# An FFT filter followed by a routed mixture of experts on one core: two input buffers, stores on ScalarE's DMA ring, a padded scratch layout, and six instead of five batches finished after the transform

## The chip, the cores and the metric

The kernel runs on one core of a Trainium2 chip. The metric is device time in microseconds (us) of one execution; the kernel before was timed three times. TensorE (PE) multiplies matrices and writes PSUM; VectorE (DVE), ScalarE (ACT) and GpSimd (POOL) work elementwise, and POOL does not read PSUM here; SyncE (SP) only issues DMAs. SP, ACT and POOL each own a DMA queue, in which their DMAs are issued in program order.

## What is computed

The input x has 8 batches of 2496 rows and 256 columns. Each column of each batch is filtered in the frequency domain, and the 19968 filtered rows then go through a layer of 8 experts with a fixed capacity of 2496 rows each:

```python
X = np.fft.rfft(x, axis=1)
y = np.fft.irfft(X * F, n=x.shape[1], axis=1)     # F = filt_r + 1j*filt_i
logits = y.reshape(B*S, D) @ w_gate
# the largest (row, expert) logits first; an expert that is full takes no more rows
h = np.maximum(x[mask] @ w1[e], 0.0)
out[mask] = h @ w2[e]
```

## The kernel before

**The transform.** 2496 is split as 39 x 64. For each batch `load_x` brings x in three DMAs (L186), one per third of the columns: 39 rows of the first index go to 39 partitions, so a third is 39 x 64 pieces of 86 numbers (344 bytes), and the tile `xt` has 117 partitions. There is one `xt` buffer (22 KB in each partition). `cp_x` (L188 to L195) turns the tile round into `xr0` and `xr1`, two copies each, on DVE (for batch 0 half of them on ACT). `s1` (L207) is the 39-point transform on PE, its results leave PSUM through ACT and DVE (L215). `s2` (L222) is the 64-point transform, followed on DVE by two products with the filter (L228, L229) and on POOL by a difference and a sum (L230, L231). `tr` (L241) transposes the product, `split` makes a high and a low part (ACT L256, DVE L257), L250 and `trv` (L263) prepare the logits. `inv1` (L271) is the first step of the inverse transform: for each q of 0 to 9 it makes a tile `zt` of two values of k1, copied out of PSUM by DVE for even q and ACT for odd q (L283), and stores it to the scratch `zd` in DRAM with two DMAs of 64 partitions (L285), on SP's queue for batches 0 to 6 and ACT's for batch 7. `zt` has 4 buffers.

**The last step.** `load_z` (L357, L359) reads `zd` back in units of five groups of 120 rows (five units per batch, the last with two groups), and `inv2` (L386 to L389) multiplies each with the constant cD (40 or 120 rows by 117), the result leaves PSUM on L390 into `xo`, and L393 stores it to the scratch `xs`, from which the experts gather their rows.

**Order.** `run` gives each call a slot and a priority, a batch being 10 slots, and writes the program in that order; a scheduler with a timing model may move instructions within it, the queues then run in order. With o = 10b, `s1` of batch b stands at slots o-10 to o, `cp_x` of the next batch at o-4.4 and o-0.3, `load_x` of batch b+2 at o-0.2, after the second `cp_x` that empties the single buffer. The last step of batches 0 and 1 stands at slots 18 to 26 and 28 to 36, that of batch 2 (`B - NPOST - 1`) at slots 75 to 83. The other NPOST = 5 batches, 25 units, are worked off in `after()` behind the transform, while the routing looks for the first expert's threshold in 11 rounds of counting (L550 to L610, PE L558 and L571). In that stretch PE's order is written by hand: `Pump` asks for a round each time enough PE work was put between, and units that are left over follow when the first 512 places are known (`for c in units: pass`, L996). The gather of the first expert's rows (L814) and its weights (L793, L999) need all stores to `xs`.

**The experts.** From there on PE multiplies gathered rows with w1 (L850) and w2 (L899), for 8 experts in turn, with the routing of the next expert beside it. The change leaves this part alone, but for two formulas of row numbers.

Memory: the pool `zp` (three `z`, two `xo` buffers) is there from the start; the pool `fx` with `xt` and `xr` is given back at slot 70.5 (`freed`).

Of the kernel before, what the change touches and what calls it, by code (L numbers as in the profile page):

```python
# [15 lines left out]
G = 22  # L16
# [3 lines left out]
NPOST = 5  # L20
# [24 lines left out]
def constants():  # L45
# [4 lines left out]
    cD = np.zeros((120, 117))  # L50
    for b in range(3):
        cS1[39*b:39*b+39, 40*b:40*b+40] = np.concatenate([c, -s], 1)
        cD[40*b:40*b+40, 39*b:39*b+39] = np.concatenate([c, -s], 1).T
# [30 lines left out]
    row[:, 32], row[:, 33], row[:, 34] = p, 64 * (p % 39) + p // 39, p // 39  # L84
# [13 lines left out]
    return dict(cS1=cS1.astype(f), cD=cD.astype(f), cW=cW.astype(f), cEh=Eh, cEl=_round(E - Eh),  # L98
# [4 lines left out]
class Fft:  # L103


    def __init__(s, tc, i, xs, zd, lg, pp, zp):
        s.tc, s.nc, s.i, s.xs, s.zd, s.lg, s.pp, s.zp = tc, tc.nc, i, xs, zd, lg, pp, zp
        s.zw = s.zo = s.y7 = None
# [124 lines left out]
    def tr(s, b, q):  # L233
# [8 lines left out]
        if b == B - 1 and q > 4:  # L242
            nc.scalar.copy(s.y7[:, 2*q:2*q+2], p)
        else:
            s.split(b, q, p, nc.vector)
        if k:
# [5 lines left out]
            nc.scalar.copy(s.vs[b, g], p)  # L252

# [19 lines left out]
    def inv1(s, b, q):  # L273

        nc = s.nc
        if (b, q) not in s.yd:
            s.split(b, q, s.y7[:, 2*q:2*q+2], nc.gpsimd)
        zt = s.wp.tile([128, 2, D], F32, name="zt", bufs=ZB)
# [5 lines left out]
        for r in range(2):  # L284
            (nc.scalar if last else nc.sync).dma_start(s.zd[b][:, 20*r+2*q:20*r+2*q+2], zt[64*r:64*r+64])  # L285
# [5 lines left out]
    def v1(s, g, b0, b1):  # L291

        nc = s.nc
        if s.y7 is None:
            s.y7 = s.wp.tile([128, K1, D], F32, name="Y1", tag="Y1", bufs=2)
# [7 lines left out]
        z = s.y7[r, :10].rearrange("p k d -> p (k d)").rearrange("p (n r k) -> p k r n", r=2, k=K1)[:, 4*g:4*g+4]  # L303
        nc.scalar.copy(z, p[:c].rearrange("p k (r n) -> p k r n", r=2))

    def v2(s, b0, b1):
# [3 lines left out]
        z = s.y7[r, :10].rearrange("p k d -> p (k d)")  # L310
        s.U = s.zp.tile([120, G, c], F32, name="xo", tag="xo", bufs=2)
        n = 8 if c > 8 else G
        for g0 in range(0, G, n):
            g1 = min(g0 + n, G)
            p = s.pt([128, g1 - g0, c], not b0)
            for g in range(g0, g1):
                m = 120 if g < 21 else 40
                nc.tensor.transpose(p[:m, g-g0], z[:, 120*g:120*g+m], s.id[r, r])
            m = min(g1, 21)
            nc.vector.tensor_copy(s.U[:, g0:m], p[:120, :m-g0])  # L320
            if g1 == G:
                nc.vector.tensor_copy(s.U[:40, 21], p[:40, 21-g0])

    def v3(s, b0, b1):
# [3 lines left out]
        for g0 in range(0, G, n):  # L328
            g1 = min(g0 + n, G)
            m = min(g1, 21)  # L330
            p = s.pt([128, g1 - g0, c], not b0)
            nc.tensor.matmul(p[:117, :m-g0], s.cD, s.U[:, g0:m], start=True, stop=True)
            if g1 == G:
                nc.tensor.matmul(p[:117, 21-g0], s.cD[:40], s.U[:40, 21], start=True, stop=True)
            nc.vector.tensor_copy(s.lg[:, b0:b1, g0:g1], p[:117].rearrange("p g (b e) -> p b g e", e=8))

    def more_z(s, units):
# [4 lines left out]
        s.xos = [y[:117, k] for k in range(4)]  # L342
# [8 lines left out]
    def load_z(s, b, t, z=None):  # L351
        g0, gf = 5*t, min(5*t+5, 21)
        if z is None:
            z = s.new_z((b, t) in s.rest)
        s.z[b, t] = z
        v = s.zd[b].rearrange("n k c -> (n k) c")
        s.nc.sync.dma_start(z[:, :gf-g0], v[120*g0:120*gf].rearrange("(g p) c -> p g c", p=120))  # L357
        if t == 4:
# [766 lines left out]
```

## Time and profile before

| what | us |
|---|---|
| median of 3 runs (1575.35 to 1582.28) | 1579.18 |
| the profiled execution, its own time | 1580.15 |
| span of that execution in the trace | 1578.4 |
| from the span's start to the first matmul of the transform | 30.65 |
| from the first matmul of the second batch to the last batch's s1 | 66.08 to 326 |
| the last batch's s1 | 326 to 377 |
| rest of the transform, to the first threshold round | 377 to 449.7 |
| threshold, 25 units of the last step, first gather | 449.7 to 533.7 |
| the experts | 533.7 to 1578 |

The table cuts the span into stages by what PE does. The profile's page gives each engine's busy time over the whole span and in 40 equal slices; the timeline gives instructions in order of time, with the idle time before them in brackets and what ended it; the waits view sums such idle time by pairs. The granted clock of PE is a share of full speed.

### The profile page before, as it was taken

The numbers are of one execution on the slowest core, as the hardware profiler recorded it, in microseconds if no ns is written. First come the engines' busy times: TensorE is split into PE (matmuls) and PEld (weight loads), VectorE is DVE, ScalarE is ACT, GpSimd is POOL, SyncE is SP. The second block draws the span as 40 slices with busy tenths as digits, with TensorE's granted clock in tenths as the row PEclk, the third lists the DMA queues.
The fourth block names the chain that finished last, engine by engine and source line by source line (L and its number), as shares of the span: only waits on it lengthen the run. The fifth ranks groups of instructions, "written<-read, shape, count | busy, mean of one in ns | idle before, by whom it ended". The sixth has DMA issues, their size and how long they took to land.

```text
span 1578.4 us, 27475 instructions
## 1 busy us (share of the span) xinstructions
PE 1419.3 (90%) x10374; PEld 1240.7 (79%) x10374; DVE 979.5 (62%) x2620; ACT 727.5 (46%) x1703; POOL 537.5 (34%) x557
## 2 busy tenths in 40 slices
PE   2788779799898689999999989999999999999998
PEld 1687658689664378888878878888879889899898
DVE  2677556588544856876776686786696772622322
ACT  4465445566444642643553453453462453632322
POOL 0233223335210242354264434343433443333311
PEclk9899989899979789999999999999999999999999
DMA  8878898845878510211121211211211221111100
GB/s 151 146 111 170 189 186 131 170 93 141 190 217 278 185 53 21 88 59 33 71 63 43 77 45 50 79 51 43 89 44 40 92 98 41 48 44 41 47 28 26
DMA packets 121096, 148.75 MB, mean 94 GB/s; under 512 B 70629, under 2 KB 93755, under 8 KB 118659
## 3 DMA queue, kind: packets, MB, share of 16 engines
q1 hardware_dynamic: 97994, 70.63, 22.6%
q0 software_dynamic: 17840, 60.34, 11.8%
q10 hardware_dynamic: 5129, 16.01, 2.9%
q8 instruction: 82, 1.34, 0.4%
q14 instruction: 51, 0.42, 0.1%
HBM read 84.47 MB, written 62.50 MB: 93 GB/s over the span
## 4 chain that ended last, share of the span: by engine, by line
PE 43%; DVE 10%; issue 7%; ACT 2%; POOL 1%; DMA 1%; another core or an unknown queue 0%; POOLq 0%; DVEq 0%; ACTq 0%
PE py L899 20%; PE pz L850 19%; PE rt L558 2%; PE ptr L828 2%; DVE hl L864 1%; POOL out L910 1%; ACT lg L718 1%; DVE hl L867 1%; DVE w0l L808 1%; DVE w1l L808 1%; DMA wr<-moe_w,widx 1%; DVE Gm L550 1%; DVE OH L749 1%; PE rt L755 1%; DVE tmp L639 0%
## 5 line engine op out<-in xcount | busy, mean ns | idle before, releaser
L899 PE MATMUL py<-w1h,hl 128*128 128x256 f32 x2496 | 485.6, 287 | 3.3 <-DVE hl L867 2.8
L899 PEld LDWEIGHTS py<-w1h,hl 128*128 128x128 f32 x2496 | 403.3, 192 | 7.5 <-DVE hl L867 3.7
L899 PE MATMUL py<-w1l,hl 128*128 128x256 f32 (+1 forms) x1280 | 360.1, 283 | 0.0
L910 POOL DMA_INDIRECT out<-y,oid x160 | 173.7, 1086 | 452.3 <-ACT y L909 410.5
L856 ACT ACTIVATE hl<-pz 128x512 fp32r<-128x512 f32 (+1 forms) x320 | 186.4, 587 | 218.1 <-PE pz L850 182.2
L850 PE MATMUL pz<-xo,w0h 128*128 128x512 f32 (+1 forms) x640 | 265.4, 415 | 12.3 <-DVE hl L864 6.7
L850 PE MATMUL pz<-xo,w0l 128*128 128x512 f32 (+1 forms) x640 | 250.1, 391 | 0.0
L850 PE MATMUL pz<-z,w0h 128*128 128x512 f32 (+1 forms) x640 | 249.3, 389 | 0.8 <-DVE z L832 0.8
L899 PEld LDWEIGHTS py<-w1l,hl 128*128 128x128 f32 (+1 forms) x1280 | 242.3, 189 | 2.0
L864 DVE SCALAR_TENSOR_TENSOR hl<-pz,hl 128x512 fp32r<-128x512 f32 x227 | 155.0, 687 | 121.0 <-ACT hl L856 119.5
L814 POOL DMA_INDIRECT xg<-xs,xid x160 | 171.4, 1071 | 134.3 <-issue 43.3
L909 ACT COPY y<-py 128x256 f32<-128x256 f32 x152 | 56.3, 371 | 294.5 <-PE py L899 254.5
L850 PEld LDWEIGHTS pz<-xo,w0h 128*128 128x128 f32 x640 | 122.7, 192 | 33.6 <-DVE hl L864 9.0
L207 PE MATMUL p<-cS,xr 117*128 117x120 f32 x688 | 102.2, 293 | 42.5 <-ACT xr L195 30.7
L850 PEld LDWEIGHTS pz<-xo,w0l 128*128 128x128 f32 x640 | 121.4, 190 | 24.1
L215 ACT COPY Y<-p 64x240 f32<-64x240 f32 (+1 forms) x304 | 116.0, 381 | 44.0 <-PE p L207 38.3
L850 PEld LDWEIGHTS pz<-z,w0h 128*128 128x128 f32 x640 | 122.3, 191 | 17.3 <-DVE z L832 1.8
L207 PEld LDWEIGHTS p<-cS,xr 117*128 117x128 f32 x688 | 94.0, 208 | 49.0 <-ACT xr L195 30.6
L230 POOL TENSOR_TENSOR P<-P 128x256 f32<-128x256 f32 x80 | 59.7, 746 | 209.6 <-DVE P L228 209.2
L550 DVE TENSOR_TENSOR Gm<-M,thr 117x1232 bf16<-117x1232 f32 (+2 forms) x80 | 104.4, 1316 | 0.2
L222 PE MATMUL p<-cW,Y 128*128 128x128 f32 x640 | 92.9, 280 | 1.3 <-DVE Q L229 1.2
L222 PEld LDWEIGHTS p<-cW,Y 128*128 128x128 f32 x640 | 82.9, 194 | 7.8 <-issue 3.7
(234 smaller groups left out, 2255.8 us busy)
## 6 DMA issues: line engine op xcount, KB each, us to landing
xt<-x SPq DMA_DIRECT2D x24, 838.5 KB
zd<-zt SPq DMA_DIRECT2D x140, 128.0 KB
z<-zd SPq DMA_DIRECT2D x26, 600.0 KB
xs<-xo SPq DMA_DIRECT2D x12, 585.0 KB
xs<-xo ACTq DMA_DIRECT2D x11, 585.0 KB
xs<-Y ACTq DMA_DIRECT2D x9, 585.0 KB
zd<-zt ACTq DMA_DIRECT2D x20, 128.0 KB
xg<-xs,xid POOLq DMA_INDIRECT x160
```

What stands on the lines that cost most here:

```text
L207: s.lastmm = nc.tensor.matmul(p[:, q-q0, :120], xv[:, q-24*h], s.cS1, start=True, stop=True).ins
L215: (nc.vector.tensor_copy if t in ((5,) if b else (1, 3, 5, 7, 9)) else nc.scalar.copy)(dst, src)
L222: nc.tensor.matmul(p[:, k], s.Y1[b][:, 4*g+k, dh*128:dh*128+128], s.cW[:, 4*g+k], start=True, stop=True)
L230: nc.gpsimd.tensor_tensor(P[:, :, :64], P[:, :, :64], P[:, :, 64:], op=OP.subtract)
L550: nc.vector.tensor_tensor(Gm[:, s0:s1, :m], s.M[:, s0:s1].unsqueeze(2).to_broadcast([117, s1 - s0, m]), thr[:117].unsqueeze(1).to_broadcas ...
L814: s.lastg = s.nc.gpsimd.indirect_dma_start(out=xg[:n], out_offset=None, in_=s.xs, in_offset=bass.IndirectOffsetOnAxis(ap=ids[0][:n, t:t+1] ...
L850: nc.tensor.matmul(p[:, :n], w[:, sl], x[:, k, :n], start=m == 0, stop=m == 5)
L856: s.lasta = nc.scalar.activation(h[:, :n], p[:, :n], AF.Relu).ins
L864: nc.vector.scalar_tensor_tensor(l[:, :n], p[:, :n], 0.0, h[:, :n].bitcast(F32), op0=OP.max, op1=OP.subtract)
L899: nc.tensor.matmul(p[:a.stop-a.start], hs[g][f][:, a], b[:, 256*f:256*f+256], start=m == 0, stop=m == 8 * len(terms) - 1, skip_group_check ...
L909: s.lasta = nc.scalar.copy(y, p).ins
L910: st = nc.gpsimd.indirect_dma_start(out=out_rows, out_offset=bass.IndirectOffsetOnAxis(ap=ids[1][:w, 4*g+t:4*g+t+1], axis=0), in_=y[:w], i ...
```

## The change

There are six parts.

- **x**: two `xt` buffers; each x is loaded in six parts, and of each third of 39 partitions 32 go in DMAs of 32 partitions, the other seven in one DMA each (one partition, 64 pieces of 344 bytes), 21 per batch. The parts of x for batch b+2 are asked for at slots o-9 to o-3. Batch 0 has three large DMAs on SP's queue and its 21 small ones on ACT's.
- **cp_x**: the first half stands at o-2 (o-4.4 before); one of the four copies of a batch moves from DVE to POOL.
- **stores**: `zt` holds four k1 and has two buffers; each pair of q is stored by two DMAs, all on ACT's queue; the stores of `xs` stand on ACT's queue throughout.
- **scratch layout**: `zd` is 40 x 66 rows, two of 66 being padding that is set to zero by eight small DMAs on SP; a unit of z is then 120 partitions with one run of 5 KB each. cD is 120 x 120, `xs` has 120 rows where it had 117, and the special case of the last group is gone.
- **the last step**: NPOST is 6. The last step of batches 0 and 1 stands at slots 62 to 69, 0.8 slots a unit, its `z` and `xo` cut out of the x buffer that is no longer used; `after()` gets 30 units.
- **memory**: `zp` is opened in `freed`.

```diff
-NPOST = 5
+NPOST = 6
...
-I1, FS, C0 = 5, -1, -4.4
+I1, C0, EZ = 5, -2, 0.8
...
-NP, NZ, MZ, NXO, ZB, NH = 5, 4, 8, 4, 4, 10
+NP, NZ, MZ, NXO, ZB, NH = 5, 4, 8, 4, 2, 10
...
-        s.nz, s.st_x = 3, tc.nc.sync
+        s.nz, s.st_x = 3, tc.nc.scalar
...
+        q = s.wp.tile([128, 4, D], F32, name="zt", bufs=ZB)
+        nc.gpsimd.memset(q[:, :2], 0.0)
+        for zd in s.zd:
+            nc.sync.dma_start(zd[:, N2:], q[:40, :2])
...
-    def load_x(s, b):
-        x = s.i['x'][b]
-        xt = s.xp.tile([128, N2, 86], F32, name="xt", bufs=1)
-        s.xt[b] = [(xt[:117], 0, N2)]
-        xv = x.rearrange("(a c) d -> a c d", c=N2)
-        for k in range(3):
-            s.nc.sync.dma_start(xt[39*k:39*k+39], xv[:, :, 85*k:85*k+86])
+    def load_x(s, b, j):
+
+        if j == 0:
+            xt = s.xp.tile([128, N2, 86], F32, name="xt", bufs=2)
+            s.xt[b] = [(xt[:117], 0, N2)]
+        xt = s.xt[b][0][0]
+        xv = s.i['x'][b].rearrange("(a c) d -> a c d", c=N2)
+        k, h = divmod(j, 2)
+        n, d = slice(32*h, 32*h+32), slice(85*k, 85*k+86)
+        if b == 0:
+            if h == 0:
+                s.nc.sync.dma_start(xt[39*k:39*k+32], xv[:32, :, d])
+            for a in range(32 + 4*h, 36 + 3*h):
+                s.nc.scalar.dma_start(xt[39*k+a:39*k+a+1], xv[a:a+1, :, d])
+            return
+        s.nc.sync.dma_start(xt[39*k:39*k+32, n], xv[:32, n, d])
+        for a in range(32 + 4*h, 36 + 3*h):
+            s.nc.sync.dma_start(xt[39*k+a:39*k+a+1], xv[a:a+1, :, d])
...
-                eng = s.nc.scalar.copy if c and b == 0 else s.nc.vector.tensor_copy
+                eng = (s.nc.scalar.copy if b == 0 else s.nc.gpsimd.tensor_copy if h else s.nc.vector.tensor_copy) if c else s.nc.vector.tensor_copy
...
-        zt = s.wp.tile([128, 2, D], F32, name="zt", bufs=ZB)
+        if q % 2 == 0:
+            s.zt = s.wp.tile([128, 4, D], F32, name="zt", bufs=ZB)
+        zt = s.zt[:, 2*(q % 2):2*(q % 2)+2]
...
-        for r in range(2):
-            (nc.scalar if last else nc.sync).dma_start(s.zd[b][:, 20*r+2*q:20*r+2*q+2], zt[64*r:64*r+64])
+        if q % 2:
+            for r in range(2):
+                nc.scalar.dma_start(s.zd[b].rearrange("a n c -> n a c")[:N2, 20*r+2*q-2:20*r+2*q+2], s.zt[64*r:64*r+64])
...
-        s.nc.sync.dma_start(z[:, :gf-g0], v[120*g0:120*gf].rearrange("(g p) c -> p g c", p=120))
-        if t == 4:
-            s.nc.sync.dma_start(z[:40, 1], v[2520:])
+        s.nc.sync.dma_start(z[:, :g1-g0], s.zd[b].rearrange("a (i g) c -> (a i) g c", i=3)[:, g0:g1])
+
+    def early(s):
+
+        x = s.xp.tile([128, N2, 86], F32, name="xt", bufs=2).rearrange("p n d -> p (n d)")
+        s.ex = [x[:120, 1280*k:1280*k+1280].rearrange("p (g d) -> p g d", d=D) for k in range(4)]
...
             if b + 2 < B:
-                at(o - 0.2, 8, s.load_x, b + 2)
+                for j in range(6):
+                    at(o - 9 + 1.2*j if b else -0.2 + 1.1*j, 8, s.load_x, b + 2, j)
...
-            for t in range(5):
-                if b < B - NPOST:
-                    z = 10*B - I2 if b == B - NPOST - 1 else o + 18
-                    at(z - 2.5 + 2*t, 6, s.load_z, b, t)
-                    at(z + 2*t, 5, s.inv2, b, t)
+        at(10*B - 20, 0, s.early)
+        for k in range(5 * (B - NPOST)):
+            at(10*B - 17.99 + EZ*(k - 2), 9, s.load_z, k // 5, k % 5)
+            at(10*B - 18 + EZ*k, 5, s.inv2, k // 5, k % 5)
...
-        zd = [dr.tile([N2, 40, D], F32, name=f"zd{b}") for b in range(B)]
-        xs = dr.tile([117 * S, D], F32, name="xs")
+        zd = [dr.tile([2 * K1, 3 * G, D], F32, name=f"zd{b}") for b in range(B)]
+        xs = dr.tile([120 * S, D], F32, name="xs")
...
+            f.zp = pool(st, "zp", side="right", reuse_waits="tile")
```

## Rows read from the trace of the kernel before

**Rows 1.** The page: busy time of the engines, then 40 equal slices of the span.
```profile
PE 1419.3 (90%) x10374; PEld 1240.7 (79%) x10374; DVE 979.5 (62%) x2620; ACT 727.5 (46%) x1703; POOL 537.5 (34%) x557
...
PE   2788779799898689999999989999999999999998
...
PEclk9899989899979789999999999999999999999999
DMA  8878898845878510211121211211211221111100
```

**Rows 2.** Windows by stage: length, PE, PEld, DVE, ACT, POOL busy (count), clock, DMA share, GB/s.
```profile
66.08:326.00 259.92, 212.79 (x1842) 190.94 (x1843) 171.94 (x267) 139.90 (x352) 76.84 (x103) 0.89 0.82 155
326.00:377.00 51.00, 50.50 (x524) 47.73 (x523) 41.82 (x71) 35.67 (x91) 22.72 (x30) 1.00 0.35 80
377.00:449.70 72.70, 64.76 (x577) 51.82 (x576) 41.26 (x82) 37.41 (x76) 22.75 (x42) 0.88 0.81 201
449.70:533.70 84.00, 67.92 (x305) 37.79 (x304) 49.37 (x197) 44.01 (x99) 9.08 (x9) 0.87 0.80 257
533.70:1578.00 1044.30, 1000.29 (x6979) 891.43 (x6979) 649.97 (x1950) 443.91 (x1029) 402.24 (x362) 0.99 0.17 55
```

**Rows 3.** Timeline of PE: start, length, instructions, [idle before, what ended it].
```profile
30.65 3.77 PE L207 MATMUL p<-cS,xr 117*128 117x120 f32 x16 [30.65 <-ACT xr L195]
...
66.08 3.77 PE L207 MATMUL p<-cS,xr 117*128 117x120 f32 x16 [9.34 <-DVE xr L195]
...
97.66 0.58 PE L271 MATMUL pa<-yh,cEh 128*128 128x256 f32 x1 [5.88 <-DVE zt L283]
...
176.24 1.09 PE L241 MATMUL pa<-fid,P 128*128 128x128 f32 x4 [7.99 <-ACT Vh L265]
...
230.07 1.12 PE L241 MATMUL pa<-fid,P 128*128 128x128 f32 x4 [9.00 <-DVE xo L390]
...
317.11 1.11 PE L241 MATMUL pa<-fid,P 128*128 128x128 f32 x4 [7.51 <-DVE zt L283]
```

**Rows 4.** Waits up to 620 us: who waited for whom: total us, times, longest.
```profile
DVE xr L195 <- DMA xt<-x: 44.9, 6, 16.5
...
ACT zt L283 <- DMA zd<-zt: 27.5, 4, 9.7
...
DVE zt L283 <- DMA zd<-zt: 14.1, 3, 9.0
```

**Rows 5.** Timeline of SP's DMA issues at the start.
```profile
1.23 12.56 SPq L186 DMA_DIRECT2D xt<-x  x3
...
24.16 0.24 SPq L148 DMA_DIRECT2D P<-filt_r  x1
...
34.01 47.56 SPq L186 DMA_DIRECT2D xt<-x  x6
```

**Rows 6.** Windows in which x alone, and stores of zt alone, are moved (columns of rows 2).
```profile
72.00:87.00 15.00, 15.00 (x149) 14.32 (x148) 11.84 (x22) 11.87 (x31) 8.75 (x13) 1.00 1.08 141
...
330.00:370.00 40.00, 40.00 (x413) 38.05 (x410) 32.76 (x57) 26.53 (x69) 18.58 (x25) 1.00 0.38 87
```

**Rows 7.** Groups by line, 66 to 326 us: busy, mean ns, idle before.
```profile
L195 DVE COPY xr<-xt 117x1536 f32<-117x1536 f32 (+1 forms) x25 | 44.6, 1822 | 21.7 <-DMA xt<-x 21.7
L230 POOL TENSOR_TENSOR P<-P 128x256 f32<-128x256 f32 x52 | 39.2, 753 | 167.9 <-DVE P L228 167.6 <-issue 0.3
...
L386 PE MATMUL pv<-z,cD 120*117 120x512 f32 (+1 forms) x48 | 20.8, 528 | 0.0
...
L390 DVE COPY xo<-pv 117x512 f32<-117x512 f32 (+1 forms) x18 | 10.1, 567 | 19.4 <-DMA xs<-xo 14.3 <-PE pv L386 5.1
```

**Rows 8.** Timeline of ACT's own queue: two stores of zt.
```profile
449.89 1.21 ACTq L285 DMA_DIRECT2D zd<-zt  x2
```

**Rows 9.** Windows with the matmuls of L386 alone: length, PE busy (count), clock, DMA share, GB/s.
```profile
377.00:449.70 72.70, 10.47 (x24) 0.88 0.81 201
449.70:533.70 84.00, 51.18 (x120) 0.87 0.80 257
```

More of the change, by code (lines that the diff above doesn't have):

```diff
@@ L83, in constants @@
     row[:, 25:32] = G * np.arange(1, 8)
-    row[:, 32], row[:, 33], row[:, 34] = p, 64 * (p % 39) + p // 39, p // 39
+    row[:, 32], row[:, 33], row[:, 34] = p, 64 * (p % 39) + G * (p // 39), p // 39
     pw = np.zeros((128, 11, 7))
@@ L242, in tr @@
         if b == B - 1 and q > 4:
-            nc.scalar.copy(s.y7[:, 2*q:2*q+2], p)
+            nc.scalar.copy(s.y7b(q), p)
         else:
@@ L252, in tr, with y7b @@
             nc.scalar.copy(s.vs[b, g], p)
+    def y7b(s, q):
+        if q == 9 and s.y9 is None:
+            s.y9 = s.wp.tile([128, 4, 128], F32, name="P", bufs=NP).rearrange("p k d -> p (k d)")
+        y = s.y7[:, 80+512*q:592+512*q] if q < 9 else s.y9
+        return y.rearrange("p (k d) -> p k d", d=D)
     def split(s, b, q, v, eng):
@@ L329, in v3 @@
             g1 = min(g0 + n, G)
[L330 removed]
             p = s.pt([128, g1 - g0, c], not b0)
[L332 to L334 removed]
+            nc.tensor.matmul(p[:120], s.cD, s.U[:, g0:g1], start=True, stop=True)
             nc.vector.tensor_copy(s.lg[:, b0:b1, g0:g1], p[:117].rearrange("p g (b e) -> p b g e", e=8))
@@ L341, in more_z @@
         y = s.wp.tile([128, 4, 5, D], F32, name="Y1", tag="Y1", bufs=2)
-        s.xos = [y[:117, k] for k in range(4)]
+        s.xos = [y[:120, k] for k in range(4)]
         zs = [f[:120, k] for k in range(4)] + [w[:120, k] for k in range(2)]
@@ L375, in inv2_parts @@
         s.nstore += n > 0
-        if k < 2:
-            xo = s.zp.tile([117, 5, D], F32, name="xo", tag="xo", bufs=2)
+        if (b, t) not in s.rest:
+            xo = s.ex[2 + (b + t) % 2]
+        elif k < 2:
+            xo = s.zp.tile([120, 5, D], F32, name="xo", tag="xo", bufs=2)
         else:
-            xo = s.zo.tile([117, 5, D], F32, name="xo", tag="xo", bufs=NXO) if s.zo else s.xos[k-2]
+            xo = s.zo.tile([120, 5, D], F32, name="xo", tag="xo", bufs=NXO) if s.zo else s.xos[k-2]
         z = s.z[b, t]
@@ L383, in inv2_parts @@
             w = min(2, g1 - g)
-            p = s.pt([128, 2, D], b == B - NPOST - 1)
-            if g + w < G:
-                nc.tensor.matmul(p[:117, :w], s.cD, z[:, g-g0:g-g0+w], start=True, stop=True)
-            else:
-                nc.tensor.matmul(p[:117, 0], s.cD, z[:, g-g0], start=True, stop=True)
-                nc.tensor.matmul(p[:117, 1], s.cD[:40], z[:40, g-g0+1], start=True, stop=True)
-            copy[n % 2](xo[:, g-g0:g-g0+w], p[:117, :w])
+            p = s.pt([128, 2, D], False)
+            nc.tensor.matmul(p[:120, :w], s.cD, z[:, g-g0:g-g0+w], start=True, stop=True)
+            copy[n % 2](xo[:, g-g0:g-g0+w], p[:120, :w])
             if g + 2 >= g1:
@@ L404, in run @@
         at(-12, 2, s.consts2)
-        at(-12, 3, s.load_x, 1)
+        for j in range(6):
+            at(-12, 3, s.load_x, 1, j)
         at(-12, 4, s.consts3)
@@ L415, in run @@
             if b + 1 < B:
-                at(o + (C0 if b else -4.4), 8, s.cp_x, b + 1, 0)
+                at(o + C0, 8, s.cp_x, b + 1, 0)
                 at(o - 0.3, 8, s.cp_x, b + 1, 1)
             if b + 2 < B:
-                at(o - 0.2, 8, s.load_x, b + 2)
+                for j in range(6):
+                    at(o - 9 + 1.2*j if b else -0.2 + 1.1*j, 8, s.load_x, b + 2, j)
             for g in range(5):
```

52 lines of the change are left out of this document (24 added, 28 removed).

## The prediction

> **What bounds the kernel now.** I read the page first. PE is busy 90% of the span, but its tenths are full only in the later 60% of the slices; in the first third they go down to 6 to 8, the granted clock falls below full speed there, and the DMA tenths stand at 8 and 9 [rows 1]. So I cut the span into stages [rows 2]. The experts' stage has PE busy 1000 of 1044 us at a clock of 0.99 and a DMA share of 0.17: the change does not reach it, and I leave its 1044 us alone. The stage from 66 to 326 us has PE busy 212.8 of 259.9 us: 47.1 us idle, and a clock of 0.89. The stage just behind it, 326 to 377, does the same kind of work with x all loaded: PE is busy 50.5 of 51 us at full clock, the DMA share 0.35. That stage is the measure of what the first could be.
>
> PE's timeline names the gaps [rows 3]: 9.34 us for the second batch's `xr`, then gaps of 5.88 to 9.00 us which end with a copy of `zt`, `xo` or a value for the logits. Behind these the waits view finds DMAs [rows 4]: DVE waited 44.9 us for x, ACT 27.5 and DVE 14.1 us for a `zt` buffer whose store had not landed. SP's timeline shows why [rows 5]: six issues of x occupied its queue for 47.56 us, with the next one ready only when the one buffer is empty, and stores of `zt` stand in that same queue. So x is late because its buffer comes free late, and the stores are late because they stand behind x.
>
> **Start.** x of batch 0 is 2.576 MB (117 x 64 x 344 bytes). The stretch with x alone moved 141 GB/s [rows 6], so it takes 18.3 us. SP began at 1.23 us [rows 5] and the first matmul came at 30.65 [rows 3]; before that lie the landing and the 3.5 us copies. The gain lies between nothing and 5 us. Its 21 small DMAs go out on ACT's queue beside the rest. Batch 1's x already started at 34.01 us [rows 5], when SP had issued the filter, so the second buffer brings it forward by little. I take 2.5 us for the first matmul of batch 1.
>
> **66 to 326 us.** The last step of batches 0 and 1 leaves this stage. Its 56 records (48 of them L386, 20.8 us [rows 7]) come off 1842 [rows 2]; 1786 remain. At the price of the dense stage, 50.5 / 524 = 0.096 us per record [rows 2], they are 172 us of PE. The mix of lines is the same, so I take this price. Whether PE can run so tightly is decided by the others. **DVE**: 171.9 us, less 10.1 for `xo` [rows 7] and less a quarter of `cp_x` (about 10 of 44.6 us [rows 7]): 152. **ACT**: 139.9 us, plus 47 stores of `zt` at 1.21 / 2 = 0.6 us of its queue [rows 8]: about 164, less some 5 for `xo`. What is queued behind a store's issue is the next PSUM copy of ACT, and PE waits for that one when both PSUM tiles are full. **POOL**: 76.8 us [rows 2] plus six copies of 117 x 1216; by L230's 753 ns for 256 columns [rows 7] at most 3.6 us each, by DVE's own about 1.6: under 99 us, hidden. **DMA**: x takes 18.3 us per batch; the stores, 2.62 MB per batch, ran at 87 GB/s for a share of 0.38 [rows 6], so 229 GB/s with all engines and 11.4 us. The sum of 30 us stands against 172 / 5.67 = 30.3 us of PE per batch (488 of 86 records of `s1` a batch): a close match, but x now has more than a batch of time in hand. I therefore add 12 us for places where DVE, ACT or a store is late: 184 us, 76 less than 259.9. The bounds are 172 (nothing is late) and 199 (twice that again).
>
> **326 to 377 us** takes the ten units of the last step. At 51.18 us for 120 records [rows 9], 2.05 us a unit plus the last group's, I take 20 us more. Each unit's load and store, 600 KB each, fall into a stretch whose DMA share was 0.35 [rows 2]; x is in by then. `early` needs only the buffer of batch 6's x, empty since slot 50.
>
> **377 to 449.7 us** loses the five units of batch 2: L386 is 10.47 us there [rows 9]. The clock of 0.88 in this stage [rows 2] says that the chain of the last batch's logits leaves gaps which these units partly fill, so the gain could be nothing; with the clock it could be 20. I take 10.5.
>
> **449.7 to 533.7 us** gets five more units, 10.7 us of PE at the price above. PE is busy 67.9 of 84 us [rows 2], so some could go into its gaps; but the extra units follow the last threshold round in PE's order, and the first gather and the weights wait for their stores. I take 10 of 0 to 16 us.
>
> **The rest.** z in runs of 5 KB, xs on 120 partitions, cD with 120 columns and uniform last groups remove a few matmuls and lighten the DMA share of 0.8 in the last two stages [rows 2]; no engine there waits for that alone, so I count nothing, at most 5 us. Eight zero-fills and some 24 more issues per x cost SP 0.24 us each [rows 5], about 6 us a batch, on a queue with nothing urgent left in it. If that cover is gone, z's loads are late next.
>
> **Sum.** -2.5 - 76 + 20 - 10.5 + 10 = -59 us on 1580.15 us, the profiled execution's own time, which is 1 us above the median of three runs: 1521 us. What this kernel's measurement can tell from no change is about 0.5%, 8 us.
>
> **Rival 1: the one-partition DMAs bind.** Each moves 22,016 bytes into one partition. No row shows such a load landing. If it shares the whole rate of 141 GB/s it costs 0.16 us, as in the sum; if it goes at one engine's share of the store stretch, 229 / 16 = 14.3 GB/s [rows 6], it costs 1.54 us, and 21 cost 32 us per batch. With 15 us for the other 96 partitions and 11.4 us of stores a batch would need up to 59 us of DMA. Against it: other DMAs may move meanwhile. The point from which it decides: batches took 259.9 / 6 = 43 us before, and with the later terms of the sum the change loses when a batch's DMA exceeds 42 us, that is when the small ones cost over 0.74 us each. At 0.8 us each, 43.4 us a batch for six batches gives about 1590 us. I give 7% to this, slower than before. At half the price, 35 us a batch, the stage takes 25 us more than I forecast: 1546 us, 13%. [...]
>
> **Rival 2: another ring, the same engines.** The stores leave SP's queue, but the DMA engines stay as full: share 0.82 in the stage [rows 2], and x is now asked for sooner. Stores that still land late keep `zt`'s waits (27.5 + 14.1 us [rows 4]), and two buffers of four k1 turn over less often than four of two. The gaps of PE that end with `zt` are 5.9 to 7.5 us each [rows 3]; four to five of them with the clock behind them are 36 us: 1557 us, 14%. For it speaks the share, against it that x has slack and a store no longer stands behind a whole x. [...]
>
> **Rival 3: x is not asked for early.** If the order on SP's queue puts x behind a DMA that waits long, one buffer's worth of overlap is lost again and 66 to 326 keeps its gaps; then only 20 us change places and I get about 1577 us. Nothing but z's loads could do that: 4%.
>
> **How the numbers follow.** Forecast 62%, rivals 1 (half) 13%, 2 14%, 3 4%, 1 (full) 7%. Faster is the first three, 0.89; same 0.04; slower 0.07. Low end: all terms at their good bound, 12 less in the long stage, 10 behind it, 2.5 at the start, 8 in the tail: 1488. The high end holds both partial rivals with 9 us above the second: 1566.
>
> **What would show it.** Right: PE's gaps between 66 us and the last batch gone, clock near 1.00 there, DVE's wait for x under 10 us, the last batch's `s1` beginning near 248 us instead of 326, the first matmul on gathered rows near 475 us instead of 533.7. Wrong: waits of `xr` for x from batch 2 on with a DMA share near 1 (rival 1); waits of `zt` for its store (rival 2); ACT as the releaser of most PE gaps (its queue was costed too low); that matmul much over 95 us behind the first threshold round (the 30 units).

## The result, and the profile after

The changed kernel takes 1570.84 us (median of 16 runs, 1563.44 to 1577.85), the kernel before 1582.55 us beside it (16 runs): a ratio of 0.9928, 95% interval 0.9911 to 0.9944. That is faster by 0.7%, 11.7 us, where 59 were forecast; the time lies 5 us above the range. Run again beside the last experiments it had 0.9926 (0.9901 to 0.9951).

The page of the changed kernel, engines and slices:

```profile
PE 1416.7 (90%) x10354; PEld 1237.7 (79%) x10354; DVE 983.8 (62%) x2611; ACT 718.8 (46%) x1703; POOL 564.0 (36%) x566
...
PE   0478889999899689989999999999999999999998
...
PEclk9989999999999789999999999999999999999999
DMA  9998978447889410211221211211211221111100
```

From the fourth slice on the PE digits of the first third rose to 8 and 9 where they had been 7 to 9, and the clock digits there are 9 but for one 8 [rows 1]. But the first slice is now empty and the second at four tenths. The stages, by the same events as before (second batch's `s1`, last batch's `s1`, first threshold round, first gathered rows; columns of rows 2):

```profile
76.58:304.00 227.42, 199.59 (x1890) 187.50 (x1890) 173.31 (x261) 139.32 (x363) 98.34 (x114) 0.96 0.85 128
304.00:377.00 73.00, 68.35 (x541) 55.95 (x542) 45.13 (x80) 37.63 (x94) 25.27 (x31) 0.93 0.53 148
377.00:426.80 49.80, 44.52 (x447) 36.17 (x446) 38.37 (x71) 20.56 (x50) 19.57 (x37) 1.00 0.84 233
426.80:525.90 99.10, 82.50 (x381) 47.86 (x381) 52.64 (x207) 53.52 (x121) 11.13 (x11) 0.90 0.89 301
525.90:1574.50 1048.60, 1004.84 (x6979) 895.05 (x6979) 650.13 (x1950) 443.64 (x1025) 402.08 (x361) 0.98 0.17 55
```

The first threshold round, L580 after and L558 before, began at 435.87 us before (449.7 of rows 2 lies 14 us behind it). Against the kernel before the stages are: up to the second batch's `s1` +10.5 (66.08 [rows 3]), the long stage -32.5 (259.92 [rows 2]), the last batch's `s1` with ten units +22.0, on to the threshold round -9.1 (58.9 before), to the first gathered rows +1.3 (97.8), experts +4. (The borders 326 and 304 lie at the last batch's copy of `xr`. By the count of s1's matmuls, 86 a batch, its own begin at 334.94 and 315.68 us; cut there, the two stages have -29.8 and +19.3.) The sum is -3.8 us, the difference of the two profiled spans (1574.5 and 1578.4); the medians differ by 8 more, which these two executions do not show.

PE's timeline (columns of rows 3):

```profile
49.15 3.59 PE L223 MATMUL p<-cS,xr 117*128 117x120 f32 x16 [49.15 <-ACT xr L211]
...
76.58 3.74 PE L223 MATMUL p<-cS,xr 117*128 117x120 f32 x16 [7.18 <-DVE xr L211]
...
117.08 0.58 PE L293 MATMUL pa<-yh,cEh 128*128 128x256 f32 x1 [7.00 <-DVE Vl L288]
...
525.91 1.75 PE L850 MATMUL ptr<-id,xg 128*128 128x128 f32 x6 [11.34 <-DMA xg<-xs,xid]
```

The first matmul is 18.5 us later [rows 3]. The gap of 7 us at 117 ends with `Vl`, a value for the logits. What lies around it is on the timelines of ACT and of DVE:

```profile
11.19 29.93 ACTq L198 DMA_DIRECT2D xt<-x  x17
...
104.09 1.59 ACT L231 COPY Y<-p 64x240 f32<-64x240 f32 x4
110.31 1.37 ACTq L310 DMA_DIRECT2D zd<-zt  x2
111.72 0.19 ACT L287 CAST Vh<-pv 128x32 fp32r<-128x32 f32 x1 [6.05 <-DMA xt<-x]
```

```profile
115.01 1.92 DVE L211 COPY xr<-xt 117x1536 f32<-117x1536 f32 x1 [7.89 <-DMA xt<-x]
...
116.84 0.18 DVE L288 TENSOR_TENSOR Vl<-pv,Vh 128x32 fp32r<-128x32 f32 x1
```

ACT had nothing to copy from 105.68 us on, stood in front of two stores until 110.31, and the cast that `Vl` needs came at 111.72. The idle time is put down to a DMA of x, not to the store. But `Vl` itself stands on DVE behind a copy of batch 2's `xr`, which waited for x until 115.01: this gap of PE is that of a late x (the DMA share from 79 to 115 us is 1.06), and ACT's wait was over before it. ACT waited in the same way three more times up to 304 us, for 5.17, 3.44 and 4.26 us; behind these PE's gaps are under 1 us each but for one of 2.48 us, which a copy on DVE ends. No wait for `zt`'s buffer of rows 4's kind is left. And 17 small DMAs of batch 0's x hold ACT's queue for 29.93 us, 1.76 us each.

### The profile page after: what moved, and what is told of

Same layout as the page of the kernel before. It is cut to its first block, busy times and chain, and to the rows that moved or that the text cites. A ratio compares the mean times of both kernels' runs of the same rounds, so it can differ in the third digit from the quotient of the medians.

```text
span 1574.5 us, 27463 instructions
## 1 busy us (share of the span) xinstructions
PE 1416.7 (90%) x10354; PEld 1237.7 (79%) x10354; DVE 983.8 (62%) x2611; ACT 718.8 (46%) x1703; POOL 564.0 (36%) x566
## 4 chain that ended last, share of the span: by engine, by line
PE 56%; DVE 14%; DMA 12%; issue 8%; ACT 4%; SPq 2%; POOL 2%; ACTq 1%; another core or an unknown queue 0%; POOLq 0%; DVEq 0%
PE py L921 21%; PE pz L872 20%; DMA xt<-x 6%; PE pv L409 4%; DMA zd<-zt 3%; PE rt L580 2%; DVE xr L211 2%; PE ptr L850 2%; PE p L238 2%; PE pa L293 2%; PE p L223 2%; ACT lg L740 1%; DVE hl L886 1%; POOL out L932 1%; DMA wr<-moe_w,widx 1%
## 5 line engine op out<-in xcount | busy, mean ns | idle before, releaser
L872 PE MATMUL pz<-xo,w0h 128*128 128x512 f32 (+1 forms) x640 | 266.9, 417 | 12.1 <-DVE hl L886 6.2
L223 PE MATMUL p<-cS,xr 117*128 117x120 f32 x688 | 97.5, 288 | 64.9 <-ACT xr L211 49.1
L223 PEld LDWEIGHTS p<-cS,xr 117*128 117x128 f32 x688 | 88.9, 202 | 70.3 <-ACT xr L211 49.1
```

The lines of the kernel that those rows point to most:

```text
L223: s.lastmm = nc.tensor.matmul(p[:, q-q0, :120], xv[:, q-24*h], s.cS1, start=True, stop=True).ins
L872: nc.tensor.matmul(p[:, :n], w[:, sl], x[:, k, :n], start=m == 0, stop=m == 5)
```

## The experiments

Each run stands against the kernel before on its own chip, so the ratios compare; 0.1% is 1.6 us. The last three columns are from each profile: first matmul, PE's matmuls between 76 and 304 us, first threshold round / first gathered rows.

| run | ratio (95%) | first | 76 to 304 | round / rows |
|---|---|---|---|---|
| before | 1 | 30.7 | 1655 | 435.9 / 533.7 |
| after | 0.9928 (0.9911-0.9944) | 49.2 | 1890 | 426.8 / 525.9 |
| E1 batch 0's x in 39s | 0.9907 (0.9876-0.9938) | 30.9 | 1858 | 420.8 / 518.6 |
| E2 batch 0's x in 32s and 7s | 0.9938 (0.9918-0.9957) | 31.2 | 1810 | 427.2 / 528.1 |
| E3 all x in six 39s | 0.9928 (0.9900-0.9957) | 31.0 | 1837 | 425.3 / 525.2 |
| E4 copy back on DVE | 0.9989 (0.9969-1.0009) | 49.2 | 1791 | 431.6 / 531.0 |
| E5 stores on SP | 0.9801 (0.9774-0.9829) | 51.4 | 2047 | 403.7 / 506.0 |
| E6 all x in three 39s | 0.9864 (0.9839-0.9890) | 31.0 | 1864 | 416.8 / 514.8 |
| E7 E6, stores on SP | 0.9909 (0.9883-0.9934) | 30.6 | 1803 | 418.3 / 517.9 |
| E8 E3, stores on POOL | 0.9956 (0.9938-0.9975) | 30.2 | 1876 | 411.2 / 523.3 |
| E9 before, stores on ACT | 1.0233 (1.0204-1.0261) | 30.6 | 1411 | 467.1 / 567.2 |
| E10 E3, stores on SP | 0.9860 (0.9837-0.9884) | 30.8 | 1948 | 407.3 / 510.0 |
| E11 E5 and E1 | 0.9794 (0.9770-0.9818) | 30.2 | 2041 | 400.2 / 501.3 |
| E12 E5, first three x in three 39s | 0.9750 (0.9724-0.9776) | 31.3 | 2033 | 395.2 / 499.2 |
| E13 E12, asked late | 0.9756 (0.9728-0.9784) | 31.0 | 2037 | 394.9 / 498.3 |
| E14 E13, one x buffer | 0.9985 (0.9968-1.0002) | 30.8 | 1852 | 428.5 / 533.5 |
| E15 E12, copy on DVE | 0.9833 (0.9805-0.9862) | 30.7 | 1943 | 405.9 / 505.4 |
| E16 E12, 25 units behind | 0.9828 (0.9795-0.9860) | 30.8 | 2030 | 420.9 / 505.4 |
| E17 E13, 35 units behind | 0.9790 (0.9770-0.9810) | 30.5 | 2058 | 382.7 / 497.9 |

**The start (E1, E2, E3).** E1:

```diff
-                s.nc.sync.dma_start(xt[39*k:39*k+32], xv[:32, :, d])
-            for a in range(32 + 4*h, 36 + 3*h):
-                s.nc.scalar.dma_start(xt[39*k+a:39*k+a+1], xv[a:a+1, :, d])
+                s.nc.sync.dma_start(xt[39*k:39*k+39], xv[:, :, d])
```

> Only batch 0's x goes back to three DMAs of 39 partitions on SP's queue; everything else is as in the changed kernel, where the first matmul came at 49.15 us. Theory A (the 21 one-partition DMAs take about 1.8 us each, one behind another, whatever is beside them): the first matmul comes near 31 us as before the change, and with the second batch's s1 following it by 27 to 36 us the kernel gains 12 to 18 us, to about 1555 us. Rival B (the start is late because batch 1's x and the filter load now compete with batch 0's x): the first matmul stays at 45 us or later and the time within 3 us of the changed kernel's.

E2, the seven partitions in one DMA, still on ACT's queue:

```diff
-            for a in range(32 + 4*h, 36 + 3*h):
-                s.nc.scalar.dma_start(xt[39*k+a:39*k+a+1], xv[a:a+1, :, d])
+            s.nc.scalar.dma_start(xt[39*k+32:39*k+39], xv[32:, :, d])
```

> Batch 0's x keeps its 32-partition DMAs on SP and the rest of it on ACT's queue, but the seven partitions of a third go in one DMA instead of seven. Theory A (a DMA into one partition is what is slow, so seven partitions in one DMA run beside each other): first matmul at 31 to 36 us, 10 to 17 us gained. Rival C (ACT's queue is what is slow at the start, because other loads and its table stand in it): first matmul stays at 44 us or later, less than 5 us gained. Together with the run that puts all of it on SP this separates the queue from the size.

E3 takes E1's edit for batch 0 and for the others:

```diff
-        s.nc.sync.dma_start(xt[39*k:39*k+32, n], xv[:32, n, d])
-        for a in range(32 + 4*h, 36 + 3*h):
-            s.nc.sync.dma_start(xt[39*k+a:39*k+a+1], xv[a:a+1, :, d])
+        s.nc.sync.dma_start(xt[39*k:39*k+39, n], xv[:, n, d])
```

> No one-partition DMA anywhere: batch 0 in three DMAs of 39 partitions, the later batches in six of 39 partitions by 32 n. Theory A (the small DMAs cost DMA time in the steady batches too): beyond the gain at the start (12 to 18 us) x of batch 2 lands earlier, DVE's wait of 7.89 us for it goes, and the stage from the second batch's s1 to the last batch's loses another 10 to 20 us: about 1540 us. Rival D (behind the start the small DMAs are hidden; batches of 36 to 44 us are set by DVE, ACT and POOL): no more than 3 us beyond the run that changes batch 0 alone, with batch spacings of 36 to 44 us as they are.

All three bring the first matmul back to 31 us: 21 DMAs of one partition made the start late, not ACT's queue as such (E2 uses it). But the kernel gets none of E2's or E3's 18 us, and E1's interval overlaps with the changed kernel's. Most of it goes at once: PE now waits for the second batch's `xr`, 18.99 us in E1, 24.78 in E2 and 15.50 in E3, and that batch's s1 begins at 75.76, 77.67 and 71.37 us, against 76.58 in the changed kernel. In E1 batch 1's x, 27 DMAs as before, begins on SP's queue at 34.52 us (31.72 in the changed kernel). A further loss is in E1's trace too, all engines in order of time:

```profile
75.76 5.00 PE L221 MATMUL p<-cS,xr 117*128 117x120 f32 x24 [18.99 <-DVE xr L209]
...
96.41 0.59 ACT L305 COPY zt<-pa 128x512 f32<-128x512 f32 x1
...
110.39 0.56 SPq L198 DMA_DIRECT2D xt<-x  x1
110.95 1.34 ACTq L308 DMA_DIRECT2D zd<-zt  x2
...
112.34 0.19 ACT L285 CAST Vh<-pv 128x32 fp32r<-128x32 f32 x1 [15.33 <-DMA xt<-x]
...
112.80 1.08 PE L264 MATMUL pv<-P,gate 128*32 128x128 f32 x16 [11.72 <-DVE Vl L286]
```

The data of the store were ready at 97.0 us; it went out at 110.95, when a DMA of x had landed. For 15 us ACT did nothing, and with it PE, DVE and POOL ran dry; here `Vl` waits for ACT's cast. In the trace's records of the DMA instructions (no view shown here) the cause can be read: the 401 DMAs of SP's and ACT's queues in the changed kernel use eight completion semaphores in turn (51 DMAs on one, 50 on each of the others), in program order over both queues, and each first waits until the DMA that used its semaphore before has landed (none of the 393 with one before them went out sooner than 16 ns behind its last update): the store issued there at 110.31 has the semaphore of a piece of x that SP had issued at 104.33 and that landed at 110.21. The store of 110.95 in E1 waits on that of a piece which SP had issued at 105.97. POOL's DMAs have eight others. With 27 DMAs per x, the DMA eight places ahead is often a piece of x (for 31 of the 48 stores that the changed kernel issued from 76 to 304 us), and it may be waiting itself. In the same records ACT stands in front of issues of its stores, from 76 to 304 us, for 15.1 us in the changed kernel, 31.8, 41.0 and 20.3 us in E1 to E3, 4.1 in E6 and not at all in E5. They explain the late start as well: the issues of the 21 small DMAs take 0.51 to 0.93 us each, and the rest of the 29.93 us are turns waited for, 10.19 us of it (14.53 to 24.72) for a load of the filter that SP had issued at 16.48.

**The stores' queue (E5, E9, E8).** E5 is the changed kernel with one word changed; E9 makes the opposite edit to the kernel before:

```diff
-                nc.scalar.dma_start(s.zd[b].rearrange(...
+                nc.sync.dma_start(s.zd[b].rearrange(...
```

```diff
-            (nc.scalar if last else nc.sync).dma_start(s.zd[b][...
+            nc.scalar.dma_start(s.zd[b][...
```

> Only the queue of the zt stores goes back from ACT to SP; 27 DMAs per x, the two buffers and everything else stay as in the changed kernel. There ACT stood up to 6.05 us behind a store's issue and was released by an x DMA (in the run with batch 0's x as before: 15.33 us). Theory G (a store on ACT's queue still waits for x DMAs issued before it, and now ACT's copies wait with it): ACT's waits released by x DMAs are gone, PE's gaps behind Vl and Q shrink, 5 to 15 us faster than the changed kernel. Rival H (stores were late in the kernel before because of SP's queue, and ACT's waits lie beside other work): zt buffers are waited for again, 5 to 20 us slower. Rival D (neither is on the path): within 3 us.

> The kernel before with one edit: all its zt stores on ACT's queue instead of SP's. Theory G (a store waits for the x DMAs ahead of it in program order on either queue, and ACT's copies wait with it): the waits for zt's buffers stay or turn into ACT waits behind the issue, released by x; 0 to 20 us slower than the kernel before, ratio 1.000 to 1.013. Rival M (SP's queue was what made the stores late, as the forecast had it): the waits of ACT (27.5 us) and DVE (14.1 us) for zt go, 10 to 30 us faster, ratio 0.981 to 0.994.

E5 is the result that decides: 0.9801, 20 us less than the changed kernel, and more than the 15 expected at most. Its gap of 9.48 us for batch 2's `xr` is still there. Without the gaps that end with `xr` or with what stands behind it on DVE (0.58 and 7.00 us in the changed kernel, 2.35 and 9.48 in E5), PE's idle time from 76 to 304 us falls from 20.8 to 7.3 us. Two windows of its long stage:

```profile
150.00:186.00 36.00, 34.20 (x346) 32.32 (x347) 31.86 (x48) 25.37 (x66) 18.56 (x22) 1.00 1.04 155
186.00:221.00 35.00, 35.00 (x358) 33.40 (x357) 29.10 (x47) 25.52 (x64) 18.53 (x21) 1.00 0.79 137
```

PE is busy 35.00 of 35 us at 0.098 us per matmul and full clock: the dense price of the forecast (0.096), in a window with x under way and a DMA share of 0.79. E9 costs 2.3%, 37 us, nearly twice the most that was expected; rival M had it faster. Its ACT timeline, and PE's:

```profile
226.01 8.74 ACTq L285 DMA_DIRECT2D zd<-zt  x2
...
234.79 0.27 ACT L252 COPY vs<-pv 128x128 f32<-128x128 f32 x1 [16.87 <-DMA zd<-zt]
```

```profile
235.10 2.06 PE L386 MATMUL pv<-z,cD 120*117 120x512 f32 x2 [14.86 <-ACT vs L252]
```

One pair of stores held ACT for 16.87 us and PE for 14.86. The profile names a store as what ended it; by the records the two issues waited for the turns of two thirds of x, issued at 205.58 and 214.67 and landed at 225.93 and 234.27, while the data to be stored had been ready at 215.53. So moving the stores to ACT costs in either kernel, though `zt` no longer stands behind x on SP.

E8 gives the stores a queue with semaphores of its own (`nc.gpsimd`, on top of E3).

> Six DMAs of 39 partitions per x, zt stores on POOL's queue, where no x DMA and no other transfer of this stage stands. Theory G: neither ACT nor SP waits for the other's DMAs; 10 stores a batch cost POOL some 10 us, which it has (12 to 13 us busy of 36 to 40 in two stages of the run with six DMAs); 5 to 15 us faster than that run, if POOL's product P is not delayed. Rival I (POOL becomes the bound, since P waits behind each store's issue): PE gaps released by POOL P L242/L243 over 1 us each, 5 to 20 us slower.

POOL's waits view of E8, 71 to 304 us (total, times, longest):

```profile
POOL zd L306 <- ACT zt L303: 20.3, 12, 5.1
```

At an issue POOL waited for data, 20.3 us, and no row of the view has it wait there for x. This fits the reading that the shared turn held ACT; that the load on the DMA engines had no part in it is not shown. The threshold round comes 14 us sooner than in E3. But behind it 112.2 us pass instead of 99.9, and the run is no faster than E3, so that neither expectation came true; what those 12 us are was not tried.

**How much x stands ahead of a store (E6, E7, E10).** E6 has no split of n, three DMAs of 39 partitions per x; E7 is E6 and E10 is E3, each with E5's edit.

> Every x goes in three DMAs of 39 partitions, as in the kernel before, instead of 27 DMAs; two buffers, early asking, and stores on ACT stay. Theory G (DMAs are let go in program order over both queues with a bounded number outstanding, so a store waits for an x DMA a few places ahead of it, and fewer x DMAs mean that this one is older): ACT's waits behind store issues fall from about 20 us (those over 2 us, to 304 us) to under 10, and with the earlier start the kernel gains 10 to 20 us over the changed one. Rival D (the number and size of the x DMAs does not matter once x is in time): like the run with six DMAs of 39 partitions, ratio 0.993 to the kernel before.

> Three DMAs of 39 partitions per x and the zt stores on SP: of the change's DMA edits only the second buffer, the early asking and the padded layout are left. Theory G (ACT's waits come from its stores): no ACT wait released by x behind an issue; the best of the DMA arrangements, 10 to 25 us faster than the changed kernel (ratio to the kernel before 0.977 to 0.987). Rival H: a store stands behind a whole third of x (6 us or more) on SP, zt's two buffers run out, and this is 5 to 15 us slower than the run with the same three DMAs and stores on ACT.

> All x in six DMAs of 39 partitions, zt stores on SP; against the run with three DMAs and stores on SP (ratio 0.9909, zt waits for stores 28.8 and 15.8 us) and the one with 27 small DMAs and stores on SP (0.9801, no such wait). Theory K (on SP a store stands behind the x DMA in front of it, so what it waits is the size of that DMA): zt waits between, 10 to 30 us, ratio 0.982 to 0.990. Rival L (it is the number of outstanding DMAs that counts, and six a batch are few enough): no zt waits, ratio 0.972 to 0.980.

With stores on ACT, three DMAs an x are better than six or 27 (0.9864 against 0.9928 twice), and ACT stands least in front of its stores there (4.1 us, as given above), as Theory G has it. With stores on SP it is the other way: 27, six, three give 0.9801, 0.9860, 0.9909. E7's waits, 76 to 304 us, show rival H:

```profile
DVE zt L300 <- DMA zd<-zt: 28.8, 5, 10.1
ACT zt L300 <- DMA zd<-zt: 15.8, 4, 6.5
```

These are the waits of rows 4 over again: a store on SP stands behind the DMA of x in front of it, and with thirds of x the two rows come to 44.6 us. Theory G's forecast for E7, the best of all, was wrong; that of K for E10 holds in the ratio, with waits of 33.6 us in the same two rows.

**The best of both (E11, E12).** No store is issued before batch 0's inverse step, so the first x can be large and the later ones small.

```diff
-        if b == 0:
+        if b < 3:
             if h == 0:
-                s.nc.sync.dma_start(xt[39*k:39*k+32], xv[:32, :, d])
-            for a in range(32 + 4*h, 36 + 3*h):
-                s.nc.scalar.dma_start(xt[39*k+a:39*k+a+1], xv[a:a+1, :, d])
+                s.nc.sync.dma_start(xt[39*k:39*k+39], xv[:, :, d])
             return
```

> zt stores on SP and only batch 0's x in three DMAs of 39 partitions. In the run of that edit with stores on ACT the first matmul came 18 us sooner, the second batch's s1 only 0.8 us sooner, and the time fell by 3 us. Theory J (batch 1's x is set by the sum of the transfers before it): again 2 to 6 us, ratio 0.976 to 0.980. Rival (with ACT free the earlier start is kept): 10 to 18 us, ratio 0.969 to 0.974.

> zt stores on SP, x of batches 0 to 2 in three DMAs of 39 partitions (no zt store is issued before batch 0's last inverse step, so none can stand behind them), x of batches 3 to 7 in 27 small DMAs as in the changed kernel. Theory G with the start as a separate loss: the first matmul comes at about 31 us instead of 51, batch 1's x copies at 61, batch 2's at 87 to 95 instead of 117, PE's gaps of 5.6 and 9.5 us in the run with stores on SP alone shrink, no zt wait for a store; 8 to 20 us faster than that run, ratio to the kernel before 0.968 to 0.975. Rival J (all transfers of the first 120 us share one rate, and the slot order, not x, sets batches 1 to 3): within 4 us of it, ratio 0.978 to 0.982.

E12 beats both kernels: 0.975, against 0.9928. With batch 0 alone (E11) the 20 us at the start are nearly lost again, as J expects: batch 1's copies began at 70.6 us (71.7 in E5), those of batch 2 at 119.4 (117.2). In E12 they began at 60.6 and 90.4.

**What the rest is worth (E13 to E17, and the changed kernel beside them).**

> The changed kernel as it is, beside the next three on one chip, so that they can be set against it without the difference between chips: ratio to the kernel before 0.991 to 0.995.

> The run with zt stores on SP and x of batches 0 to 2 in three DMAs, with one edit: the parts of x for batch b+2 are asked for at slots o-0.2 to o+5.3 for every b (o-9 to o-3 before), which is where a single buffer would let them. If x on time was the main term of the forecast (the idle PE of 66 to 326 us), x is waited for again before most batches and it is 20 to 50 us slower than that run (ratio 0.988 to 1.005). If the gain is the stores' and the moved last step's, within 6 us (0.972 to 0.979).

E13 tells nothing of early asking: SP issued x at nearly the same times (178.69 us against 178.95 for the same piece), so the slots in the source did not set its order. E14 does what E13 meant to do:

```diff
-            xt = s.xp.tile([128, N2, 86], F32, name="xt", bufs=2)
+            xt = s.xp.tile([128, N2, 86], F32, name="xt", bufs=1)
...
-        x = s.xp.tile([128, N2, 86], F32, name="xt", bufs=2).rearrange("p n d -> p (n d)")
+        x = s.xp.tile([128, N2, 86], F32, name="xe", bufs=1).rearrange("p n d -> p (n d)")
```

> The run with late asking, with one x buffer instead of two (the last step of batches 0 and 1 gets the other 22 KB from the start under a name of its own). The late asking had changed nothing (ratio 0.9756 against 0.975), and SP's issues of x stood at nearly the same times in both. If the second buffer carries the main term of the forecast (x on time), each x can only start when the copies of the one before are done, 18 us or more of load lie between, PE's gaps behind xr return in most batches and the time is 20 to 50 us longer (ratio 0.988 to 1.008). If the loss of the kernel before was the stores behind x and the last step in the middle, 0 to 8 us longer (0.975 to 0.981).

E14 loses 2.3%, 36 us. PE's timeline in it has one gap per batch, and DVE's the same wait ahead of the copies of `xr`:

```profile
146.24 1.08 PE L264 MATMUL pv<-P,gate 128*32 128x128 f32 x16 [9.02 <-DVE Vl L286]
...
190.09 1.08 PE L264 MATMUL pv<-P,gate 128*32 128x128 f32 x16 [7.99 <-DVE Vl L286]
...
234.67 1.08 PE L264 MATMUL pv<-P,gate 128*32 128x128 f32 x16 [8.26 <-DVE Vl L286]
...
278.61 1.08 PE L264 MATMUL pv<-P,gate 128*32 128x128 f32 x16 [7.71 <-DVE Vl L286]
```

```profile
142.34 3.74 DVE L209 COPY xr<-xt 117x1536 f32<-117x1536 f32 x2 [9.27 <-DMA xe<-zd]
...
186.19 3.75 DVE L209 COPY xr<-xt 117x1536 f32<-117x1536 f32 x2 [8.02 <-DMA zd<-zt]
```

The profile names other DMAs that share the semaphores; by the records the last pieces of x landed at 142.12 and 185.87 us, just before each copy. So the gain hangs on the second buffer: with one buffer the rest of the change, stores on SP included, is no faster than the kernel before. What a second buffer alone gives the kernel before was not run.

E4 and E15 put POOL's copy of `xr` back on DVE, in the changed kernel and in E12:

```diff
-                eng = (s.nc.scalar.copy if b == 0 else s.nc.gpsimd.tensor_copy if h else s.nc.vector.tensor_copy) if c else s.nc.vector.tensor_copy
+                eng = s.nc.scalar.copy if c and b == 0 else s.nc.vector.tensor_copy
```

> The one copy of xr per batch that went to POOL returns to DVE. In the changed kernel the two copies run at one time, DVE's taking 4.2 to 4.4 us where 1.6 us was seen before, so DVE's time for both is no less. Theory E (POOL and DVE disturb each other, and PE's gaps of 1 to 2.5 us behind a copy come from that): DVE's copy falls back to 1.6 us, the pair takes 3.2 us, and six batches gain 0.5 to 2 us each, 3 to 12 us in all. Rival F (the copy on POOL does relieve DVE, which is the bound of a batch): 5 to 12 us slower. In between (within 3 us): the copies lie on no path.

> The same run (stores on SP, first three x in three DMAs) with the POOL copy of xr back on DVE. With ACT's waits still there this edit was some 0.6% slower. If that came from DVE being next to the bound (172 us of work in 240), it is again 4 to 10 us slower (ratio 0.978 to 0.982); if it came from where ACT's stalls fell, within 4 us; if the two engines' copies disturb each other more than they save (4.36 and 2.96 us at one time against 3.2 us in a row), 3 to 8 us faster (0.970 to 0.973).

Both lose, 0.6 and 0.8%. That the two engines disturb each other is true all the same (last section). In E15 the threshold round comes 10.7 us later than in E12; why so much for one copy of 1.6 us a batch stays open.

E16 sets `NPOST = 5` and `EZ = 0.55` in E12, E17 `NPOST = 7` in E13.

> The same run with 25 units of the last step behind the transform instead of 30 (batch 2's five units join the ten in place of x, 0.55 slots a unit). The forecast priced five units behind the transform at 10 us, and the changed kernel showed 1.3 us from the first threshold round to the first gathered rows (97.8 to 99.1). If the price is hidden behind the threshold rounds, that stretch stays at 98 to 104 us and the first round comes later by what the units cost PE, 10 us: 5 to 12 us slower (ratio 0.978 to 0.983). If the gap of 11 us ahead of the first gathered rows is the price, it falls to 6 us, and the time is within 5 us.

> The run with late asking, with 35 units of the last step behind the transform instead of 30: only batch 0's five stand in place of x. From 25 to 30 units the stretch from the first threshold round to the first gathered rows grew from 84.5 to 104 us and the first round came 25.7 us sooner. If that exchange goes on, the first round comes 8 to 12 us sooner and the stretch grows by 10 to 20: within 8 us either way (ratio 0.971 to 0.981). If the gap of 11 us ahead of the first gathered rows is set by the stores of the last units, it stays at 11 us or grows by up to 5.

From round to gathered rows 25, 30 and 35 units take 84.5, 103.5 to 104.0 and 115.2 us, and the round comes at 420.9, 395 and 382.7. From 30 to 35 the exchange is 11.7 against 12.1 us: nothing is hidden and nothing gained. From 25 to 30 it is 19.5 against 25.8: the transform loses more than the stretch behind it gains. E16 also packs its 15 units closer (0.55 slots), so the two are not separated. Both readings expected of E16 missed this; its gap ahead of the gathered rows did fall, to 7.78 us.

## Why the prediction was wrong

The direction was right, and so was one half of the mechanism: x was late because its one buffer came free late. E14 shows what the second buffer is worth with the stores on SP, 36 us. The other half was wrong: the stores did not leave SP's queue at no price, and the small DMAs did not go unnoticed.

**ACT's queue, the step that failed.** The forecast priced the stores on ACT at 0.6 us of its queue each and said that the next PSUM copy is queued behind them, then hid both in ACT's slack. It priced the issue and not the wait ahead of it. That wait is mostly for a DMA of x, up to 6.05 us in the changed kernel and 15.33 in E1, where PE stood 11.72 us behind it. E5 measures the whole of it: 20 us.

**Start.** Forecast -2.5, measured +10.5. "Its 21 small DMAs go out on ACT's queue beside the rest" had no price; they made the first matmul 18.5 us later, though the second batch's s1, for which x of batch 1 decides, only 10.5. The forecast had 24 more issues per x cost SP about 6 us a batch "on a queue with nothing urgent left in it"; batch 1's x held that queue for 30.57 us where its three DMAs had taken 11.99 before the change, and batch 2's came 7.89 us late for DVE. E11 and E12 show what x of batches 1 and 2 costs with the start: together 8 us, though the intervals of E5 and E12 touch.

**66 to 326 us.** Forecast 184, measured 227.4. Of the 43.4 us, 10 are 104 more matmuls than the 1786 forecast (x 0.096): work came forward, and is paid back later. 17 are the price, 199.59 / 1890 = 0.106 us at a clock of 0.96. 16 are idle time, 27.8 instead of 12. PE does run at about the dense price in E5's windows from 150 to 221 us (69.20 us for 704 matmuls, 0.098), but not over the whole stage, where E5 has 208.85 us for 2047, 0.102.

**326 to 377** went as forecast: +22 for 20, of which the units' matmuls are 20.22. **The tail** gained 9.1 for 10.5. **Behind the threshold round** the forecast was +10, measured +1.3. The price was right (E17: 11.7 for five units); but PE had 381 matmuls left at the round and before the change 375, so that the five units had been made up by work done ahead of it, at a clock of 0.90 instead of 0.81 over these stretches:

```profile
435.87:533.70 97.83, 78.77 (x375) 47.24 (x371) 52.32 (x208) 49.22 (x108) 10.35 (x10) 0.81 0.79 250
```

(the kernel before, columns of rows 2). The gap ahead of the gathered rows grew from 5.87 to 11.34 us.

**What stays open.** E12, with the stores and the first loads mended, gains 2.5%, 40 us, where 59 were forecast. Its threshold round comes 40.7 us sooner than before the change; the forecast's terms up to there make 69. Between 76 and 304 us it needs 206.01 us for 2033 matmuls, 0.101 each, and is idle for 22; what keeps it from the dense price there was not tried. Three slips of the working change neither the sum nor the range: 139.9 + 47 x 0.6 is 168 and not 164, the bound of 199 us does not follow from "twice that again", and rival 1 at its full price gives 1597 by the sum's own terms, not 1590.

**The rivals.** Rival 1 was right in the first batches and not behind them: its sign, a wait of `xr` for x at a DMA share near 1, came once, for batch 2; E3 and E10, without a small DMA, are no faster than the changed kernel and E5. The 1.76 us per DMA at the start lie near its 1.54 and over the 0.74 from which it was to decide, but by luck: they are not the price of a small DMA alone, since most of them are turns waited for. No run measures a small DMA by itself, so the 0.8 us each, from which this rival's 1590 us is added up, is shown by none; what the runs show is issues of 0.51 to 0.93 us and the waits ahead of them. E2, with seven partitions per DMA, took the delay away, but it changes the number of DMAs and their width at once; the waits for turns speak for the number.

Rival 2 (1557 for 1570.84) came nearest in its reason, that the move to another queue does not help, but with the wrong wait: not `zt`'s buffers but ACT itself. In the runs the move to ACT's queue did not only fail to help: it cost 20 us (E5) and 37 us (E9), because the engine that issues has work of its own behind the issue.

Rival 3, x not asked for early, is nearest in its number, 1577, by chance: it did not come to pass. DVE's wait for x behind the first two batches is a single one of 7.89 us, and E14 shows what a wait in every batch looks like.

## What to carry to other kernels

Before a DMA moves to a compute engine's queue, ask what its issue waits for, not what it costs: here the DMAs of two queues shared eight completion semaphores in turn, a small store waited for the DMA eight places ahead, often a load, and so did every copy behind it (15.1 us in front of stores in the changed kernel, 41.0 in E2). In these runs large loads were best where no store stood behind them (0.9750 in E12, 0.9801 in E5), small pieces where stores shared their queue (0.9801 in E5, 0.9860 and 0.9909 in E10 and E7). And an edit of several parts should be taken apart: here one part, taken out, cost 36 us, and another, taken out, gave 20.

## What the runs showed of the hardware

DVE and POOL get in each other's way in these copies. The changed kernel's timeline, both engines:

```profile
192.13 2.96 POOL L211 COPY xr<-xt 117x1216 f32<-117x1216 f32 x1
192.13 4.36 DVE L211 COPY xr<-xt 117x1216 f32<-117x1216 f32 x1
```

and that of E5, where DVE was first:

```profile
123.94 1.61 DVE L211 COPY xr<-xt 117x1216 f32<-117x1216 f32 x1
124.09 4.22 POOL L211 COPY xr<-xt 117x1216 f32<-117x1216 f32 x1
```

With none on POOL the copy takes 1.59 to 1.99 us on DVE (15 of them in the kernel before). In the changed kernel's batches from the third on, where one such copy runs on each engine at one time, POOL took 2.96 us and DVE 3.46 to 4.36 in five pairs, and DVE's copy ended 1.40 us behind POOL's in each; in the sixth, at 310.95, DVE took 1.61 and POOL 4.30, much as in E5's rows above. What sets the order is in no row. Even so the copy was worth having on POOL: back on DVE it cost 0.6 and 0.8% (E4, E15).

The same x (2.576 MB) in 27 DMAs held SP's queue for 23.3 to 27.2 us, first issue to last, in the changed kernel's batches from the third on, and in three DMAs 14.02 us (E13, at 63.28).
